# The value product of an attention stage from one float32 pass to three float16 passes

## The chip, the core and the metric

The kernel runs on one core of a Trainium2 chip. Its time is device microseconds of that core, the median of several runs; the profile is of one execution. The core's engines each work through their own instructions in order: TensorE (PE, with its weight loads as PEld), VectorE (DVE), ScalarE (ACT), GpSimd (POOL) and SyncE (SP, which issues most transfers).

## What is computed

Attention with rotary embedding over 4 batches, 8 heads, 576 positions and head size 64, then two feed-forward stages over the 2304 x 512 result: one that takes the maximum of three products, and one with x * sigmoid(x).

```python
scores = scale * np.matmul(q_rot, k_rot.transpose(0, 1, 3, 2))
scores = scores - np.max(scores, axis=-1, keepdims=True)
attn = np.exp(scores)
attn = attn / (np.sum(attn, axis=-1, keepdims=True) + 1e-09)
attn_out = np.matmul(attn, v)
...
h = np.maximum(np.maximum(x @ w1, x @ w2), x @ w3)
x = h @ w_out
...
h = x @ w_in
g = h * (1.0 / (1.0 + np.exp(-h)))
out = g @ w_out
```

## The kernel before

The attention takes the heads in pairs: 4 batches x 4 pairs. A pair's 576 queries are cut in two parts, 256 queries (two tiles of 128) and 320 (two tiles of 128 and a last one, t == 4, with the 64 left queries of both heads). That makes 20 tiles in a batch and 80 in all, and `attention` (line 480) runs them as a software pipeline with one step for each tile: the scores of tile j go to PSUM (`tile_scores`), VectorE takes their maximum (L374) and ScalarE the exponential with its sum (L381), both in `tile_max`; `tile_norm` scales tile j-1 by its sum (L390 to L393); `tile_turn` transposes the probabilities of tile j-2 on TensorE, three 128 x 128 blocks to a PSUM bank (L422; L408, L413 and L414 for the last tile), and copies each bank into the SBUF tile `pt`. Of these copies two in three are ScalarE's (L426) and one VectorE's (L428). The bank ring `ps_t` has two banks, which the turns of q and k (`qk_turn`) use as well. When a part's tiles are all turned, one step later, `av` multiplies: `xp`, one bank, gets the product of a part by one matmul of all 128 columns of the array (L437, the 64 last keys of both heads) and eight of 64 columns (L441, four blocks of keys for each of two heads, the heads in the two halves of the columns). All are float32, and each float32 matmul stands in the trace as two MATMUL records. ScalarE then writes the high float16 part of `xp` (L444) and VectorE the rest (L445); these feed the first feed-forward stage.

`load_v` brings a pair's values into a ring of six float32 tiles `vd`; `v_max` and `v_scale` measure a batch's largest value and make a power of two of it, which scales `xp` at L444 and L445. Work that is not part of the tile pipeline is put at a step by `at(step, function)`: the loads and rotations of q and k, the loads and maxima of v, and `av`.

Between the attention's steps the program places matmul groups of the first feed-forward stage (`moe1`, matmuls at L510, float16 in three passes), as soon as the batch's part is ready (`x_ready`) and at a rate of 8000 columns a step; and work that brings the weights to float16 parts (`narrowing`, `narrow_w2`, `Weights.split`, on POOL, DVE and ACT). The order of each engine's instructions is then made by a scheduler that simulates the program. After the attention come what is left of the first stage and all of the second (L778, L809). Of the second stage nothing is changed.

Of the kernel before, what the change touches and what calls it, by code (L numbers as in the profile page):

```python
# [7 lines left out]
F32 = mybir.dt.float32  # L8
F16 = mybir.dt.float16
I32 = mybir.dt.int32  # L10
U16 = mybir.dt.uint16
AF = mybir.ActivationFunctionType
ALU = mybir.AluOpType
# [4 lines left out]
P = 128  # L18
# [4 lines left out]
def fused_kernel(  # L23
# [22 lines left out]
    nc = tc.nc  # L46
    B, H, S, D = q.shape
    NP = H // 2
# [34 lines left out]
    once = right("once", 1)  # L83
# [8 lines left out]
    pt_p = right("pt", 2)  # L92
# [5 lines left out]
    cos_sb = once.tile([P, 9, D], F32, name="cos_sb")  # L98
    sin_sb = once.tile([P, 9, D], F32, name="sin_sb")

    NK, NV = 4, 6
    qd = [once.tile([P, P], F32, name=f"qd{i}") for i in range(NK)]
    kd = [once.tile([P, P], F32, name=f"kd{i}") for i in range(NK)]
    vd = [once.tile([P, 5, P], F32, name=f"vd{i}") for i in range(NV)]
    yscr = dram.tile([P, KC, NT], F32, name="yscr")

    zscr = {nm: dram.tile([P, KC * (F2 // 512) * 512], F32, name="z" + nm) for nm in ("wi", "wo")}
# [2 lines left out]
    def all_max(m):  # L110

        ps = ps_m.tile([P, 512], F32, tag="m", name="m")
        nc.tensor.transpose(ps[0:1, 0:P], m, ident)
        t = small.tile([1, 1], F32, tag="amax", name="amax")
        nc.vector.tensor_reduce(out=t, in_=ps[0:1, 0:P], op=ALU.max, axis=AX.X)
        nc.tensor.matmul(ps[:, 256:257], ones, t, start=True, stop=True)
        return ps[:, 256:257]

    def scale_of(m, n, nm, pool=None):

        pool = pool or small
        e = pool.tile([P, n], F32, tag=nm + "e", name=nm + "e")
        s = pool.tile([P, n], F32, tag=nm + "s", name=nm + "s")
        i = pool.tile([P, n], F32, tag=nm + "i", name=nm + "i")
        ei, si, ii = e.bitcast(I32), s.bitcast(I32), i.bitcast(I32)
        nc.vector.tensor_scalar(out=e, in0=m, scalar1=2.0 ** -45, scalar2=None, op0=ALU.max)
        nc.vector.tensor_scalar(out=ei, in0=ei, scalar1=EXPMASK, scalar2=None, op0=ALU.bitwise_and)
        nc.vector.tensor_scalar(out=si, in0=ei, scalar1=-1, scalar2=267 << 23, op0=ALU.mult, op1=ALU.add)
        nc.vector.tensor_scalar(out=ii, in0=ei, scalar1=13 << 23, scalar2=None, op0=ALU.subtract)
        return s, i  # L130
# [17 lines left out]
    def flat(t):  # L148
        return t.rearrange("p a b -> p (a b)")

    def split(h, l, x, s, engine="act"):

        if engine == "act":
            nc.scalar.activation(out=h, in_=x, func=AF.Copy, scale=s)
        elif engine == "pool":
            nc.gpsimd.tensor_scalar(out=h, in0=x, scalar1=s, scalar2=1.0, op0=ALU.mult, op1=ALU.mult)  # L156
        else:
            nc.vector.tensor_scalar(out=h, in0=x, scalar1=s, scalar2=None, op0=ALU.mult)
        nc.vector.scalar_tensor_tensor(out=l, in0=x, scalar=s, in1=h, op0=ALU.mult, op1=ALU.subtract)
# [85 lines left out]
    raw_t, T_t, v_t, x_t = {}, {}, {}, {}  # L245
    sv_t, cy_t = {}, {}
# [30 lines left out]

    def load_v(b, hp):

        t = vd[(NP * b + hp) % NV]  # L280
        src = v[b, 2 * hp:2 * hp + 2]
        nc.sync.dma_start(
            out=t[:, 0:4, :].rearrange("p a x -> p (a x)").rearrange("p (h c d) -> p h c d", h=2, c=4),
            in_=src[:, 0:512, :].rearrange("h (p c) d -> p h c d", c=4),
        )
        for g in range(2):
            nc.sync.dma_start(out=t[64 * g:64 * g + 64, 4, 64 * g:64 * g + 64], in_=src[g, 512:576, :])
        v_t[b, hp] = t
# [9 lines left out]
    def v_scale(b):  # L298
        ma = vmax_t.pop(b)
        m = small.tile([P, 1], F32, tag="vm1", name="vm1")  # L300
        nc.vector.tensor_reduce(out=m, in_=ma, op=ALU.max, axis=AX.X)
        sv_t[b] = scale_of(all_max(m), 1, "v")

    def qk_rope(b, hp, eng=None):
        t = raw_t[b, hp]
# [38 lines left out]

    s_t, e_t, sum_t, pt_t, exps = {}, {}, {}, {}, []
    HK = (slice(0, 576), slice(576, 1152))
    evacs = [0]

    def tile_scores(key):
        b, hp, t = key  # L350
# [16 lines left out]
    def heads(key):  # L367
        return 1 if key[2] == 4 else 2
# [18 lines left out]
    def tile_norm(key):  # L387
        e, m = e_t[key], heads(key)
        r = small.tile([P, 2], F32, tag="rec", name="rec")
        nc.scalar.activation(out=r[:, 0:m], in_=sum_t.pop(key)[:, 0:m], func=AF.Copy, bias=1e-9)  # L390
        nc.vector.reciprocal(out=r[:, 0:m], in_=r[:, 0:m])  # L391
        for g in range(m):
            nc.scalar.activation(out=e[:, HK[g]], in_=e[:, HK[g]], func=AF.Copy, scale=r[:, g:g + 1])  # L393

    def tile_turn(key):
        b, hp, t = key
        n = P
        e = e_t.pop(key)
        r = int(t > 1)
        q0, w = PARTS[r][:2]  # L400
        if (b, hp, r) not in pt_t:
            pt_t[b, hp, r] = pt_p.tile([P, 9, w], F32, tag="pt", name="pt")
        pt = pt_t[b, hp, r]
        o = P * t - q0
        if t == 4:
            tr = ps_t.tile([P, 512], F32, tag="tr", name="tr")
            for c in range(4):
                nc.tensor.transpose(tr[:, c * P:(c + 1) * P], e[:, c * P:(c + 1) * P], ident)  # L408
            t4 = tr.rearrange("p (c g q) -> p c g q", c=4, g=2)
            nc.scalar.activation(out=pt[:, 0:4, o:o + 64], in_=t4[:, :, 0], func=AF.Copy)  # L410
            nc.vector.tensor_copy(out=pt[:, 5:9, o:o + 64], in_=t4[:, :, 1])
            tr = ps_t.tile([P, 512], F32, tag="tr", name="tr")
            nc.tensor.transpose(tr[:, 0:P], e[:, 448:576], ident)  # L413
            nc.tensor.transpose(tr[0:64, P:2 * P], e[:, 512:576], ident)  # L414
            nc.scalar.activation(out=pt[0:64, 4, o:o + 64], in_=tr[0:64, P:P + 64], func=AF.Copy)
            nc.vector.tensor_copy(out=pt[64:128, 4, o:o + 64], in_=tr[64:128, 64:128])
            return
        for j in range(3):
            tr = ps_t.tile([P, 512], F32, tag="tr", name="tr")
            for i in range(3):  # L420
                c = 3 * j + i
                nc.tensor.transpose(tr[:, i * n:(i + 1) * n], e[0:n, c * P:(c + 1) * P], ident[0:n, 0:n])  # L422
            to, of = pt[:, 3 * j:3 * j + 3, o:o + n], tr[:, 0:3 * n].rearrange("p (a n) -> p a n", a=3)
            evacs[0] += 1
            if evacs[0] % 3:
                nc.scalar.activation(out=to, in_=of, func=AF.Copy)  # L426
            else:
                nc.vector.tensor_copy(out=to, in_=of)  # L428

    def av(b, hp, r):  # L430
        if hp == 0 and r == 0:
            x_t[b] = x_p[b % 2].tile([P, NP, 2, S], F16, tag="x", name="x")
        pt, vv = pt_t.pop((b, hp, r)), v_t[b, hp]
        o, n = PARTS[r][:2]
        v4 = vv[:, 0:4, :].rearrange("p a x -> p (a x)").rearrange("p (h c d) -> p h c d", h=2, c=4)
        xp = ps_x.tile([P, 512], F32, tag="xp", name="xp")
        nc.tensor.matmul(xp[:, 0:n], vv[:, 4, :], pt[:, 4, :], start=True, stop=False)  # L437
        for c in range(4):
            for g in range(2):
                r = slice(64 * g, 64 * g + 64)  # L440
                nc.tensor.matmul(xp[r, 0:n], v4[:, g, c, :], pt[:, c + 5 * g, :], start=False, stop=(c == 3))  # L441
        xh, xl = x_t[b][:, hp, 0, o:o + n], x_t[b][:, hp, 1, o:o + n]
        sv = sv_t[b][0]
        nc.scalar.activation(out=xh, in_=xp[:, 0:n], func=AF.Copy, scale=sv)  # L444
        nc.vector.scalar_tensor_tensor(  # L445
            out=xl, in0=xp[:, 0:n], scalar=sv, in1=xh, op0=ALU.mult, op1=ALU.subtract
        )

    pairs = [(b, hp) for b in range(B) for hp in range(NP)]
# [7 lines left out]
    def at(j, f, *a):  # L457
        events.setdefault(j, []).append((f, a))
# [6 lines left out]
    for i, (b, hp) in enumerate(pairs):  # L465
        u = first[b, hp]
# [6 lines left out]
    for b in range(1, B):  # L473
        u = first[b, 0]
        for hp in range(NP):
            at(u - 10 + hp if hp < 2 else u - 4, load_v, b, hp)
            at(u - 2, v_max, b, hp)
        at(u, v_scale, b)

    def attention():  # L480

# [217 lines left out]
    o = 0  # L699
    while o < NT:  # L700
        n = min(512, NT - o)
# [195 lines left out]
    for hp in range(NP):  # L897
        load_v(0, hp)
# [6 lines left out]
    for hp in range(NP):  # L905
        at(1, v_max, 0, hp)
    at(2, v_scale, 0)

    def moe_groups():
        for b in range(B):  # L910
            for half, cols, down in moe1(b, mpools):
                if down and b not in cy_t:
                    pre_down()
                    y_scale(b)
                yield b, half, cols
# [48 lines left out]
    n = 0  # L964
# [63 lines left out]
```

## Time and profile before

| | us |
|---|---|
| median of 3 runs | 1076.05 |
| lowest and highest run | 1074.24, 1076.91 |
| the profiled execution's own time | 1072.23 |
| its span, first to last instruction | 1070.5 |
| attention, first to last maximum (L374) | about 26 to 626 us of the span |

The profile gives each engine's busy time, the span in slices, the chain of work that ended last, groups of instructions by line, and waits. A duration of a matmul record runs to its modelled end; matmuls overlap, so the pace of a stream is read from the starts.

### The profile page before, as it was taken

How to read it: one execution, taken by the hardware profiler on the slowest of the kernel's cores; microseconds unless marked ns; L12 is line 12 of the kernel's file. 1: busy time of each engine (PE TensorE's matmuls, PEld its weight loads, DVE VectorE, ACT ScalarE, POOL GpSimd, SP SyncE). 2: the span in 40 equal slices, each digit the busy share in tenths (PEclk: the TensorE clock that was granted, in tenths of full speed). 3: DMA queues.
4: the chain of work that ended last, by engine and by line, in shares of the span. 5: the costliest groups of instructions: out<-in, count | busy, mean ns of one | idle time of the engine just before them, and what ended most of it. 6: DMA issues, size and time to landing. Idle time of an engine off the chain costs nothing.

```text
span 1070.5 us, 19191 instructions
## 1 busy us (share of the span) xinstructions
PE 984.0 (92%) x7554; PEld 761.6 (71%) x7554; DVE 595.0 (56%) x1078; ACT 592.0 (55%) x1298; POOL 370.2 (35%) x396
## 2 busy tenths in 40 slices
PE   2378897999998999989999999999999999999997
PEld 1245574676776677667767567778888888888887
DVE  5858667544476666476456559654532533533432
ACT  3668775646665767756666756464433433433432
POOL 1596125730115741032111211144343433433432
PEclk9678998999999999999999999998999999999999
DMA  7633022310225433223323326110100200100000
GB/s 193 204 111 111 30 90 57 82 24 1 73 85 146 122 95 90 72 73 86 122 60 89 115 68 248 49 64 1 60 10 12 60 16 6 40 21 1 21 21 20
DMA packets 81129, 76.28 MB, mean 71 GB/s; under 512 B 44944, under 2 KB 61840, under 8 KB 80528
## 3 DMA queue, kind: packets, MB, share of 16 engines
q1 hardware_dynamic: 77328, 64.77, 20.7%
q10 hardware_dynamic: 3712, 10.29, 2.9%
q8 instruction: 59, 0.97, 0.4%
q14 instruction: 30, 0.25, 0.1%
HBM read 57.21 MB, written 17.83 MB: 70 GB/s over the span
## 4 chain that ended last, share of the span: by engine, by line
PE 71%; DVE 5%; DMA 3%; POOL 1%; issue 1%; SPq 1%; ACT 1%; DVEq 0%; POOLq 0%; ACTq 0%
PE m L510 18%; PE mb L778 8%; PE m L778 8%; PE xp L441 5%; PE a L809 4%; PE c L809 4%; PE s L364 4%; PE b L809 4%; PE tr L422 4%; PE mg L510 3%; PE d L809 2%; PE xp L437 1%; PE s L361 1%; PE tr L328 1%; PE s L354 1%
## 5 line engine op out<-in xcount | busy, mean ns | idle before, releaser
L785 POOL TENSOR_TENSOR gs<-gs 128x256 f32<-128x256 f32 x144 | 131.4, 913 | 222.0 <-ACT gs L779 216.5
L510 PE MATMUL m<-x,w 128*128 128x256 f16 (+1 forms) x1380 | 197.8, 289 | 6.0 <-DVE t L528 3.2
L510 PEld LDWEIGHTS <-w 128*128 128x128 f16 x1632 | 158.6, 99 | 53.1 <-issue 13.0
L791 DVE SCALAR_TENSOR_TENSOR g<-gs,sg,g 128x768 f16<-128x768 f32 x72 | 97.9, 1362 | 173.4 <-ACT g L790 173.0
L778 PEld LDWEIGHTS <-wi 128*128 128x128 f16 x1656 | 162.0, 98 | 18.7
L809 PEld LDWEIGHTS <-g 128*128 128x128 f16 x1485 | 146.1, 99 | 21.5 <-DVE g L791 3.3
L207 POOL TENSOR_SCALAR z<-z 128x256 uint16<-128x256 uint16 x64 | 54.2, 847 | 256.6 <-DVE z L206 242.1
L374 DVE TENSOR_REDUCE nb<-s 128x2 f32<-128x1152 f32 (+1 forms) x80 | 98.7, 1234 | 63.1 <-PE s L364 48.4
L381 ACT ACTIVATE e<-s,nb 128x576 f32<-128x576 f32 x144 | 105.3, 737 | 46.3 <-DVE nb L374 42.0
L790 ACT ACTIVATE g<-gs,sg 128x768 f16<-128x768 f32 x72 | 74.9, 1041 | 72.2 <-POOL gs L785 71.1
L393 ACT ACTIVATE e<-e,rec 128x576 f32<-128x576 f32 x144 | 104.3, 768 | 17.9 <-DVE rec L391 17.7
L422 PE MATMUL tr<-ident,e 128*128 128x128 f32 x576 | 98.0, 287 | 12.1 <-ACT pt L426 3.1
L778 PE MATMUL mb<-yt,wi 128*128 128x256 f16 x828 | 95.0, 273 | 0.0
L778 PE MATMUL m<-yt,wi 128*128 128x256 f16 x828 | 94.8, 273 | 0.0
L422 PEld LDWEIGHTS tr<-ident,e 128*128 128x128 f32 x576 | 68.6, 145 | 32.8 <-ACT pt L426 5.8
L426 ACT ACTIVATE pt<-tr 128x384 f32<-128x384 f32 x128 | 61.1, 488 | 50.2 <-PE tr L422 49.8
L441 PE MATMUL xp<-pt,vd 128*64 128x256 f32 (+1 forms) x512 | 85.3, 427 | 0.0
L364 PE MATMUL s<-T 64*128 64x512 f32 (+2 forms) x384 | 82.1, 510 | 0.0
L510 PE MATMUL m<-h,wo 128*128 128x256 f16 (+1 forms) x448 | 64.9, 286 | 2.3 <-POOL wo L156 1.2
L364 PEld LDWEIGHTS s<-T 64*128 64x128 f32 x384 | 45.9, 196 | 27.3 <-issue 5.6
L779 ACT ACTIVATE gs<-mb,ch 128x512 f32<-128x512 f32 x36 | 24.7, 686 | 71.9 <-PE mb L778 71.9
L441 PEld LDWEIGHTS xp<-pt,vd 128*64 128x64 f32 x512 | 37.1, 140 | 35.0 <-issue 17.7
(199 smaller groups left out, 1500.0 us busy)
## 6 DMA issues: line engine op xcount, KB each, us to landing
z<-in_moe_w_in_dram SPq DMA_DIRECT2D x32, 256.0 KB, 3.2
z<-in_moe_w_out_dram SPq DMA_DIRECT2D x32, 256.0 KB, 3.2
w<-in_moe_w_dram ACTq DMA_DIRECT2D x6, 768.0 KB, 7.5
wo<-in_moe_w_dram ACTq DMA_DIRECT2D x6, 768.0 KB, 5.5
qk<-in_q_dram SPq DMA_DIRECT2D x32, 128.0 KB, 3.1
qk<-in_k_dram SPq DMA_DIRECT2D x32, 128.0 KB, 3.0
vd<-in_v_dram SPq DMA_DIRECT2D x16, 256.0 KB, 3.0
zwi<-z SPq DMA_DIRECT2D x32, 128.0 KB, 3.1
```

What stands on the lines that cost most here:

```text
L364: nc.tensor.matmul(s[0:n, o:o + m], qs[r], kt[r, a:a + m], start=True, stop=True)
L374: x = nc.vector.tensor_reduce(out=nb[:, 0:m], in_=s[:, 0:576 * m].rearrange("p (h k) -> p h k", h=m), op=ALU.max, axis=AX.X, negate=True)
L381: x = nc.scalar.activation(out=e[:, HK[g]], in_=s[:, HK[g]], func=AF.Exp, bias=nb[:, g:g + 1], accum_out=sm[:, g:g + 1])
L393: nc.scalar.activation(out=e[:, HK[g]], in_=e[:, HK[g]], func=AF.Copy, scale=r[:, g:g + 1])
L422: nc.tensor.transpose(tr[:, i * n:(i + 1) * n], e[0:n, c * P:(c + 1) * P], ident[0:n, 0:n])
L441: nc.tensor.matmul(xp[r, 0:n], v4[:, g, c, :], pt[:, c + 5 * g, :], start=False, stop=(c == 3))
L510: nc.tensor.matmul(ps[:, 0:n], l, r, start=(i == 0), stop=(i == len(passes) - 1))
L778: nc.tensor.matmul(ps[:, e * 256:e * 256 + 256], l, r, start=(i == 0), stop=(i == len(passes) - 1))
L785: nc.gpsimd.tensor_tensor(out=g[o], in0=g[x], in1=g[y], op=op)
L790: nc.scalar.activation(out=h, in_=x, func=AF.Copy, scale=sg)
L791: nc.vector.scalar_tensor_tensor(out=l, in0=x, scalar=sg, in1=h, op0=ALU.mult, op1=ALU.subtract)
L809: x = nc.tensor.matmul(ps, l, r, start=first, stop=last_, skip_group_check=True)
```

## The change

The value product becomes three float16 passes: high values by high probabilities, high by low, low by high. A new step `v_split` scales a pair's values and splits them into two float16 tiles (`vs`, a ring of six), on ScalarE and VectorE, at the batch's first two steps (for the first batch at steps 2 and 3); the ring of float32 tiles `vd` shrinks to four, and `v_scale` comes one step earlier. The probabilities are scaled up by 2 to the 14th through the reciprocal of their sum. Behind each turn, a new `turned` takes the bank out twice: ScalarE copies it as float16 (the high part), and VectorE then reads the same bank and subtracts that copy (the low part). So each bank has a ScalarE instruction and, behind it, a VectorE instruction, where it had one or the other. `av` has three matmuls in place of one float32 matmul, 27 instead of 9, and its results are scaled by a constant instead of a tile.

```diff
--- before.py
+++ after.py
@@ -98,10 +98,12 @@
     cos_sb = once.tile([P, 9, D], F32, name="cos_sb")
     sin_sb = once.tile([P, 9, D], F32, name="sin_sb")
 
-    NK, NV = 4, 6
+    NK, NV, NVR = 4, 6, 4
+    PSC = 2.0 ** 14
     qd = [once.tile([P, P], F32, name=f"qd{i}") for i in range(NK)]
     kd = [once.tile([P, P], F32, name=f"kd{i}") for i in range(NK)]
-    vd = [once.tile([P, 5, P], F32, name=f"vd{i}") for i in range(NV)]
+    vd = [once.tile([P, 5, P], F32, name=f"vd{i}") for i in range(NVR)]
+    vs = [once.tile([P, 2, 5, P], F16, name=f"vs{i}") for i in range(NV)]
     yscr = dram.tile([P, KC, NT], F32, name="yscr")
 
     zscr = {nm: dram.tile([P, KC * (F2 // 512) * 512], F32, name="z" + nm) for nm in ("wi", "wo")}
@@ -277,7 +279,7 @@
 
     def load_v(b, hp):
 
-        t = vd[(NP * b + hp) % NV]
+        t = vd[(NP * b + hp) % NVR]
         src = v[b, 2 * hp:2 * hp + 2]
         nc.sync.dma_start(
             out=t[:, 0:4, :].rearrange("p a x -> p (a x)").rearrange("p (h c d) -> p h c d", h=2, c=4),
@@ -300,6 +302,13 @@
         m = small.tile([P, 1], F32, tag="vm1", name="vm1")
         nc.vector.tensor_reduce(out=m, in_=ma, op=ALU.max, axis=AX.X)
         sv_t[b] = scale_of(all_max(m), 1, "v")
+
+    def v_split(b, hp):
+
+        x, t = flat(v_t[b, hp]), vs[(NP * b + hp) % NV]
+        h, l = (t[:, i].rearrange("p a x -> p (a x)") for i in range(2))
+        split(h, l, x, sv_t[b][0])
+        v_t[b, hp] = t
 
     def qk_rope(b, hp, eng=None):
         t = raw_t[b, hp]
@@ -344,7 +353,6 @@
 
     s_t, e_t, sum_t, pt_t, exps = {}, {}, {}, {}, []
     HK = (slice(0, 576), slice(576, 1152))
-    evacs = [0]
 
     def tile_scores(key):
         b, hp, t = key
@@ -387,10 +395,16 @@
     def tile_norm(key):
         e, m = e_t[key], heads(key)
         r = small.tile([P, 2], F32, tag="rec", name="rec")
-        nc.scalar.activation(out=r[:, 0:m], in_=sum_t.pop(key)[:, 0:m], func=AF.Copy, bias=1e-9)
+        nc.scalar.activation(out=r[:, 0:m], in_=sum_t.pop(key)[:, 0:m], func=AF.Copy, scale=1.0 / PSC, bias=1e-9 / PSC)
         nc.vector.reciprocal(out=r[:, 0:m], in_=r[:, 0:m])
         for g in range(m):
             nc.scalar.activation(out=e[:, HK[g]], in_=e[:, HK[g]], func=AF.Copy, scale=r[:, g:g + 1])
+
+    def turned(to, of):
+
+        h, l = to
+        nc.scalar.activation(out=h, in_=of, func=AF.Copy)
+        nc.vector.tensor_tensor(out=l, in0=of, in1=h, op=ALU.subtract)
 
     def tile_turn(key):
         b, hp, t = key
@@ -399,7 +413,7 @@
         r = int(t > 1)
         q0, w = PARTS[r][:2]
         if (b, hp, r) not in pt_t:
-            pt_t[b, hp, r] = pt_p.tile([P, 9, w], F32, tag="pt", name="pt")
+            pt_t[b, hp, r] = pt_p.tile([P, 2, 9, w], F16, tag="pt", name="pt")
         pt = pt_t[b, hp, r]
         o = P * t - q0
         if t == 4:
@@ -407,43 +421,40 @@
             for c in range(4):
                 nc.tensor.transpose(tr[:, c * P:(c + 1) * P], e[:, c * P:(c + 1) * P], ident)
             t4 = tr.rearrange("p (c g q) -> p c g q", c=4, g=2)
-            nc.scalar.activation(out=pt[:, 0:4, o:o + 64], in_=t4[:, :, 0], func=AF.Copy)
-            nc.vector.tensor_copy(out=pt[:, 5:9, o:o + 64], in_=t4[:, :, 1])
+            for g in range(2):
+                turned([pt[:, i, 5 * g:5 * g + 4, o:o + 64] for i in range(2)], t4[:, :, g])
             tr = ps_t.tile([P, 512], F32, tag="tr", name="tr")
             nc.tensor.transpose(tr[:, 0:P], e[:, 448:576], ident)
             nc.tensor.transpose(tr[0:64, P:2 * P], e[:, 512:576], ident)
-            nc.scalar.activation(out=pt[0:64, 4, o:o + 64], in_=tr[0:64, P:P + 64], func=AF.Copy)
-            nc.vector.tensor_copy(out=pt[64:128, 4, o:o + 64], in_=tr[64:128, 64:128])
+            turned([pt[0:64, i, 4, o:o + 64] for i in range(2)], tr[0:64, P:P + 64])
+            turned([pt[64:128, i, 4, o:o + 64] for i in range(2)], tr[64:128, 64:128])
             return
         for j in range(3):
             tr = ps_t.tile([P, 512], F32, tag="tr", name="tr")
             for i in range(3):
                 c = 3 * j + i
                 nc.tensor.transpose(tr[:, i * n:(i + 1) * n], e[0:n, c * P:(c + 1) * P], ident[0:n, 0:n])
-            to, of = pt[:, 3 * j:3 * j + 3, o:o + n], tr[:, 0:3 * n].rearrange("p (a n) -> p a n", a=3)
-            evacs[0] += 1
-            if evacs[0] % 3:
-                nc.scalar.activation(out=to, in_=of, func=AF.Copy)
-            else:
-                nc.vector.tensor_copy(out=to, in_=of)
+            turned([pt[:, i, 3 * j:3 * j + 3, o:o + n] for i in range(2)], tr[:, 0:3 * n].rearrange("p (a n) -> p a n", a=3))
 
     def av(b, hp, r):
         if hp == 0 and r == 0:
             x_t[b] = x_p[b % 2].tile([P, NP, 2, S], F16, tag="x", name="x")
         pt, vv = pt_t.pop((b, hp, r)), v_t[b, hp]
         o, n = PARTS[r][:2]
-        v4 = vv[:, 0:4, :].rearrange("p a x -> p (a x)").rearrange("p (h c d) -> p h c d", h=2, c=4)
+        v4 = [vv[:, i, 0:4, :].rearrange("p a x -> p (a x)").rearrange("p (h c d) -> p h c d", h=2, c=4) for i in range(2)]
         xp = ps_x.tile([P, 512], F32, tag="xp", name="xp")
-        nc.tensor.matmul(xp[:, 0:n], vv[:, 4, :], pt[:, 4, :], start=True, stop=False)
+        three = ((0, 0), (0, 1), (1, 0))
+        for i, (x, y) in enumerate(three):
+            nc.tensor.matmul(xp[:, 0:n], vv[:, x, 4, :], pt[:, y, 4, :], start=(i == 0), stop=False)
         for c in range(4):
-            for g in range(2):
-                r = slice(64 * g, 64 * g + 64)
-                nc.tensor.matmul(xp[r, 0:n], v4[:, g, c, :], pt[:, c + 5 * g, :], start=False, stop=(c == 3))
+            for i, (x, y) in enumerate(three):
+                for g in range(2):
+                    r = slice(64 * g, 64 * g + 64)
+                    nc.tensor.matmul(xp[r, 0:n], v4[x][:, g, c, :], pt[:, y, c + 5 * g, :], start=False, stop=(c == 3 and i == 2))
         xh, xl = x_t[b][:, hp, 0, o:o + n], x_t[b][:, hp, 1, o:o + n]
-        sv = sv_t[b][0]
-        nc.scalar.activation(out=xh, in_=xp[:, 0:n], func=AF.Copy, scale=sv)
+        nc.scalar.activation(out=xh, in_=xp[:, 0:n], func=AF.Copy, scale=1.0 / PSC)
         nc.vector.scalar_tensor_tensor(
-            out=xl, in0=xp[:, 0:n], scalar=sv, in1=xh, op0=ALU.mult, op1=ALU.subtract
+            out=xl, in0=xp[:, 0:n], scalar=1.0 / PSC, in1=xh, op0=ALU.mult, op1=ALU.subtract
         )
 
     pairs = [(b, hp) for b in range(B) for hp in range(NP)]
@@ -475,7 +486,9 @@
         for hp in range(NP):
             at(u - 10 + hp if hp < 2 else u - 4, load_v, b, hp)
             at(u - 2, v_max, b, hp)
-        at(u, v_scale, b)
+        at(u - 1, v_scale, b)
+        for hp in range(NP):
+            at(u + (hp > 1), v_split, b, hp)
 
     def attention():
 
@@ -905,6 +918,8 @@
     for hp in range(NP):
         at(1, v_max, 0, hp)
     at(2, v_scale, 0)
+    for hp in range(NP):
+        at(2 + hp // 2, v_split, 0, hp)
 
     def moe_groups():
         for b in range(B):
```

## Rows read from the trace of the kernel before

**Rows 1.** Page: the chain that ended last, share of the span by engine.
```profile
PE 71%; DVE 5%; DMA 3%; POOL 1%; issue 1%; SPq 1%; ACT 1%; DVEq 0%; POOLq 0%; ACTq 0%
```
**Rows 2.** Busy time in stretches: from:to and length, engines' busy us, granted clock, DMA.
```profile
20.00:60.00 40.00, 20.57 (x74) 13.86 (x74) 33.96 (x48) 21.79 (x51) 20.07 (x13) 0.66 0.58 166
60.00:120.00 60.00, 46.48 (x249) 28.05 (x249) 40.52 (x66) 47.60 (x107) 37.27 (x31) 0.89 0.33 103
120.00:200.00 80.00, 71.16 (x489) 49.36 (x489) 58.67 (x121) 52.71 (x134) 34.04 (x34) 0.96 0.23 62
200.00:640.00 440.00, 423.46 (x3004) 302.44 (x3004) 254.63 (x574) 281.70 (x759) 120.09 (x130) 0.99 0.29 83
```
**Rows 3.** Timeline of PE: start us, us, what. Each value product and the matmul behind it.
```profile
233.52 0.60 PE L437 MATMUL xp<-pt,vd 128*128 128x256 f32 x2
...
235.93 1.26 PE L510 MATMUL m<-x,w 128*128 128x320 f16 x8
...
280.31 0.70 PE L437 MATMUL xp<-pt,vd 128*128 128x320 f32 x2
...
283.25 0.45 PE L510 MATMUL m<-h,wo1f 128*128 128x320 f16 x2
```
**Rows 4.** The chain in order of time: start us, us, what. Float16 matmuls.
```profile
358.30 1.63 PE m L510 x12
...
363.32 1.31 PE m L510 x12
```
**Rows 5.** Busy time in stretches, instructions on `xp` alone: PE, PEld, DVE, ACT.
```profile
60.00:120.00 60.00, 15.49 (x71) 7.07 (x70) 1.91 (x4) 1.89 (x4) 0.89 0.33 103
120.00:200.00 80.00, 14.20 (x72) 5.97 (x72) 2.19 (x4) 2.09 (x4) 0.96 0.23 62
```
**Rows 6.** Groups by line and shape, ACT and DVE: busy us, mean ns; idle before.
```profile
L426 ACT ACTIVATE pt<-tr 128x384 f32<-128x384 f32 x128 | 61.1, 488 | 50.2 <-PE tr L422 49.8
L428 DVE COPY pt<-tr 128x384 f32<-128x384 f32 x64 | 35.2, 551 | 16.9 <-PE tr L422 16.6
L528 DVE SCALAR_TENSOR_TENSOR t<-m,t 128x320 f32<-128x320 f32 x40 | 19.5, 486 | 21.5 <-PE m L510 20.1 <-ACT t L526 1.0 <-PE tr L422 0.3
L528 DVE SCALAR_TENSOR_TENSOR t<-m,t 128x256 f32<-128x256 f32 x41 | 17.1, 416 | 6.7 <-PE m L510 4.5 <-PE m L113 1.3 <-ACT t L526 0.6
L411 DVE COPY pt<-tr 128x256 f32<-128x256 f32 x16 | 6.7, 421 | 8.4 <-ACT pt L410 8.2
L159 DVE SCALAR_TENSOR_TENSOR yt<-yr,ys,yt 128x512 f16<-128x512 f32 x16 | 12.7, 802 | 0.0
L159 DVE SCALAR_TENSOR_TENSOR w<-w,sw11s 128x768 f16<-128x768 f32 x6 | 6.1, 1010 | 1.6 <-POOL w L156 1.6
L790 ACT ACTIVATE g<-gs,sg 128x768 f16<-128x768 f32 x36 | 33.6, 935 | 1.1
```
**Rows 7.** Busy time in 20 us stretches, 120 to 640, columns as in Rows 2.
```profile
120.00:140.00 20.00, 18.61 (x141) 14.11 (x142) 16.27 (x32) 12.47 (x33) 5.45 (x6) 1.00 0.07 17
140.00:160.00 20.00, 20.00 (x152) 14.87 (x151) 12.81 (x25) 16.08 (x40) 4.18 (x3) 1.00 0.35 113
...
200.00:220.00 20.00, 19.01 (x143) 13.95 (x142) 8.62 (x14) 11.45 (x29) 12.26 (x13) 1.00 0.38 104
...
460.00:480.00 20.00, 16.12 (x128) 12.79 (x126) 15.07 (x33) 11.28 (x32) 8.13 (x9) 0.99 0.30 84
...
600.00:620.00 20.00, 17.42 (x103) 10.49 (x100) 13.15 (x34) 15.60 (x46) 4.73 (x6) 1.00 0.34 101
620.00:640.00 20.00, 18.89 (x154) 14.66 (x153) 9.72 (x32) 10.70 (x27) 1.13 (x2) 1.00 0.17 54
```
**Rows 8.** Waits of the whole span: who for whom, us, times, longest.
```profile
DVE x L445 <- ACT x L444: 17.1, 14, 2.6
```
**Rows 9.** The weight loads of the value product: duration ns min/median/max, first and last start us.
```profile
L441 PEld LDWEIGHTS xp<-pt,vd x512: 132/137/231, 61.4 to 640.7; 128*64 128x64 f32 x171
L437 PEld LDWEIGHTS xp<-pt,vd x64: 186/192/338, 58.9 to 638.4; 128*128 128x128 f32 x64
```

## The prediction

> **What bounds the kernel now.** First the chain of work that ended last: 71% of the span is PE, VectorE has 5%, ScalarE 1% [rows 1]. Then the busy time by stretch, which says where that holds [rows 2]. From 200 to 640 us, most of the attention, PE is busy 423.5 of 440 us at a granted clock of 0.99, while VectorE is at 58% and ScalarE at 64%: the matmul groups of the first feed-forward stage fill PE between the attention's steps, and PE sets the pace. Before 200 us it doesn't. From 20 to 60 PE works half the time and VectorE 85%; from 60 to 120 PE has 77%, ScalarE 79% and VectorE 68%; from 120 to 200 PE has 89% and VectorE 73%. There the weights are brought to float16, the feed-forward groups aren't ready or only just are, and the steps go as fast as VectorE, ScalarE and the transfers let them. So the question is what the change takes from PE behind 200 us and what it puts on VectorE ahead of it and beside it.
>
> **What PE saves.** A product of 256 queries takes from 233.52 to the next matmul at 235.93, 2.41 us; one of 320 takes 280.31 to 283.25, 2.94 us [rows 3]. Twelve float16 matmuls take 1.31 us at 256 columns and 1.63 at 320 [rows 4]: a step of 0.109 and 0.136 us. A float32 record is two such steps: two records on the whole array and sixteen in eight pairs, both halves of the columns at once, are 10 x 2 steps, 2.18 and 2.72 us; the other 0.23 and 0.22 are the changes between whole array and halves, which stay. Three float16 passes are 3 steps and 12 pairs, 15 steps. So a product saves five steps, 0.55 or 0.68 us, and 32 products 19.6 us. Four products of 256 lie before 120 us and four of 320 between 120 and 200 [rows 5]; the 24 left lie where PE sets the pace and save 12 x 0.55 + 12 x 0.68 = 14.7 us. The others save 4.9 us where PE mostly waits anyway.
>
> No float16 matmul of half the array stands in the trace. Its bounds: a pair in one step, as the float32 pairs go, or one after the other, two steps. I take the pair, since the row of the same form is the nearest; the other end is a rival.
>
> The weight loads speak on the side of the other end. Loading 64 columns takes 137 ns and 128 columns 192 [rows 9], 55 ns for 64 columns, and the two loads of a pair now hide under a step of 0.22 or more; the step shrinks to half. The Trainium skill, TensorEngine Tiling (Array Packing), section Restrictions and Gotchas, says that tiling the columns excludes the fast weight load, so float16 would load halves no faster than float32 does. If the two loads of a pair go one behind the other, that is 2 x 55 = 110 ns by the rows: the length of the shorter step, so by the rule as by the row the sum stays.
>
> **What VectorE gets.** All 192 banks of full tiles now end with a VectorE subtraction 384 wide from PSUM; 64 of them had a VectorE copy of 551 ns. The nearest row with a PSUM and an SBUF input is L528, 416 ns at 256 and 486 at 320, 1.09 ns an element: 556 ns at 384. 192 x 0.556 - 64 x 0.551 = 71.5 us. A last tile (16 of them) has two subtractions of 256 for a copy of 421 ns, +0.41 us, and two small ones for a small copy, about +0.3 by my estimate from the same slope: 11 us. The new split of v, 16 times 640 wide, lies between 802 ns at 512 and 1010 at 768: 0.91, 14.5 us [rows 6]. Sum: 97 us on VectorE, 82.5 of them in the turns, 1.03 us a tile.
>
> **What ScalarE gets.** 64 more copies of 488 ns, the last tiles' second copies (some 9 us, priced as VectorE's), and 16 splits of under 935 ns: 55 us at most [rows 6]. It gets less than VectorE, so I price VectorE. POOL clears two tiles fewer; SP's loads of v keep their steps, and their ring is free once the split has run, earlier than before: both nothing. `v_scale` moves up a step with its small PE and VectorE instructions; the split behind it has three steps until the batch's first product (in the first batch one or two), so its latency is hidden, and its 3.6 us a batch are counted above. Without that cover the first product would start late by them, once a batch.
>
> **Where it falls.** By 120 us four parts of two tiles have been multiplied and about ten tiles turned; four parts of three tiles follow by 200 [rows 5]. So VectorE gets 10 x 1.03 + 3.6 = 14 us in 20 to 120, 12 x 1.03 + 3.6 = 16 in 120 to 200, and 67 in 200 to 640.
>
> In 20 to 120 VectorE is busy 74.5 of 100 us [rows 2]. The cost lies between nothing, if all goes into its 25 idle us, and 14 us. I take half, 7: the first 40 us, at 85%, have little room, the rest has some.
>
> In 120 to 200 it would need 58.7 + 16 = 75 of 80 us. The highest share it holds over a long stretch is the 85% of 20 to 60 [rows 2]; at that, 75 us take 88: +8 at most, 0 at least. I take 5, nearer the upper end, since PE waits there already and its own saving of 2.7 us there is not counted.
>
> In 200 to 640 the price is what PE waits more. I sorted the 26 stretches of 20 us between 120 and 640 by VectorE's busy time [rows 7]. Twelve under 12 us (first 200 to 220, last 620 to 640): PE idle 0.2 us on average. Ten from 12 to 15 (first 140 to 160, last 600 to 620): 1.2. Four over 15 (first 120 to 140, last 460 to 480): 2.7. Of the 22 stretches behind 200, 12, 8 and 2 are of these kinds. 67 us more are 3 us a stretch; 4, 8 and 10 would be, and PE's idle time would go from 16.5 to 0.7 + 9.8 + 27.3 = 38 us: +21. That is the upper end, because stretches with a busy VectorE are also those where loads and weights are late. The lower end is 0. I take half, 10, because at 12 to 15 us half of the stretches still have PE busy without a break.
>
> Why VectorE's share should hurt at all: each of the 224 subtractions waits for ScalarE's copy of the same bank, and what stands behind it on VectorE waits too: the next tile's maximum (L374), on which the exponential and through the only score tile the next scores on PE depend, and the feed-forward stage's copies (L528), on which its two PSUM banks depend. The one pair of this form, L444 and L445, made VectorE wait 17.1 us in 14 of 32 cases [rows 8]. The transposes' two banks are held for two instructions instead of one, so PE's turns wait for them as well.
>
> **Sum.** +7 + 5 + 10 - 14.7 = +7.3 us. Behind 640 us nothing changes. The profiled execution took 1072.2 us, so 1079.5; the median of the runs shown is 3.8 above it: 1083 us.
>
> **Rivals.** The cover holds. VectorE at (254.6 + 67) / 426 = 76% and ScalarE at 74% are less than what the busiest long stretch shows, and the scheduler can order the feed-forward copies first. Then PE keeps its 14.7 us, waits 2 more behind 200 us, and the early stretches cost 2: -11, 1065 us. Against it stand the stretches over 15 us, all four with PE idle. This is the one on the other side; it decides if a VectorE busy three quarters of the time leaves PE's idle time where it is.
>
> VectorE sets the pace. All upper ends: +14 + 8 + 21 - 14.7 = +28, 1104 us. For it: 224 more waits behind ScalarE on an engine in order. Against it: the wait shrinks when VectorE comes later anyway.
>
> The halves don't overlap in float16, or their loads don't hide. Then a product is 3 + 24 = 27 steps against 20, +0.76 or +0.95 us; the 28 products behind 120 us add 12 x 0.76 + 16 x 0.95 = 24 us, with the early 7 and 5 +36: 1112 us. Against it is the float32 pace, which needs both halves at once.
>
> **How the numbers follow.** Forecast 0.42, cover holds 0.36, VectorE sets the pace 0.15, halves apart 0.07. What a measurement of this kernel can tell from no change is about 0.3%, 3.2 us. The forecast, by itself 1075 to 1092, has 0.09 inside that band; the cover's case, 1058 to 1075, has 0.06. So faster 0.30, same 0.15, slower 0.55. The range goes from 1060, the cover's case with nearly all of PE's 14.7 us, to 1106, just over the case of VectorE's pace; the halves apart stay out.
>
> **What would show it.** The product's steps: the start of L437 to the matmul behind its last half, 1.87 and 2.26 us; 2.9 or more means the halves run apart. The subtraction: mean 0.52 to 0.60 us. Early: the step at which the eighth product is done, now just before 200 us, some 12 us later. Late: PE's idle time in the 440 us of the attention's main part, 26 instead of 16.5, with waits for the subtraction's bank or L528 among its longest. I am wrong if VectorE comes to 76% there and PE's idle time stays, or if the steps before 200 us keep their times.

## The result and the profile after

The changed kernel takes 1092.5 us (median; 1090.0 to 1094.6) against 1076.5: 1.0145 times as long, with a 95% interval of 1.0107 to 1.0183. The forecast was 1083, slower, in a range of 1060 to 1106. The profiled execution took 1090.0 us with a span of 1088.2, 17.7 more than before.

The page of the changed kernel, busy time and the chain by engine:

```profile
PE 973.6 (89%) x7842; PEld 774.7 (71%) x7842; DVE 672.4 (62%) x1254; ACT 634.0 (58%) x1410; POOL 378.1 (35%) x394
...
PE 70%; DVE 7%; ACT 5%; DMA 3%; issue 2%; POOL 1%; SPq 1%; DVEq 0%; ACTq 0%; POOLq 0%
```

PE was busy 984.0 of 1070.5 us before and is 973.6 of 1088.2 now: 10 us less busy time, 28 us more idle time. VectorE is busy 77 us longer, ScalarE 42. In the chain VectorE and ScalarE have grown from 5% and 1% [rows 1] to 7% and 5%.

Busy time in the same stretches as in [rows 2], PE, PEld, DVE, ACT, POOL, then the granted clock (as a share of 2.4 GHz):

```profile
20.00:60.00 40.00, 18.32 (x63) 12.03 (x64) 34.18 (x47) 20.14 (x48) 17.86 (x12) 0.62 0.52 146
60.00:120.00 60.00, 38.29 (x221) 25.10 (x222) 47.24 (x73) 44.31 (x99) 41.77 (x33) 0.78 0.40 126
120.00:200.00 80.00, 68.08 (x517) 51.16 (x515) 64.23 (x143) 60.49 (x149) 26.08 (x24) 0.91 0.16 50
200.00:640.00 440.00, 411.03 (x3174) 306.02 (x3175) 308.76 (x695) 315.56 (x854) 131.96 (x140) 0.97 0.28 82
```

PE idles 29.0 us between 200 and 640, where it idled 16.5, and 55.3 us between 20 and 200, where it idled 41.8. The granted clock is lower in all four stretches, most from 60 to 120: 0.78 instead of 0.89.

The timeline of PE shows a product of each size (start us, us, what), as [rows 3] do for the float32 ones:

```profile
214.47 0.43 PE L448 MATMUL xp<-pt,vs 128*128 128x320 f16 x2
214.84 1.82 PE L453 MATMUL xp<-pt,vs 128*64 128x320 f16 x24
216.59 0.49 PE L369 MATMUL s<-kd,T 128*128 128x128 f32 x2
...
253.66 0.38 PE L448 MATMUL xp<-pt,vs 128*128 128x256 f16 x2
253.97 1.50 PE L453 MATMUL xp<-pt,vs 128*64 128x256 f16 x24
255.40 0.49 PE L369 MATMUL s<-kd,T 128*128 128x128 f32 x2
```

Two of the three whole-array matmuls and all 24 halves take 2.12 us at 320 and 1.74 at 256; with the third (0.136 and 0.109, it was issued a little earlier) 2.26 and 1.85. The halves do run in pairs.

The product at 214.47 is the eighth, the last of the first batch. In the kernel before it stands here:

```profile
192.00 0.70 PE L437 MATMUL xp<-pt,vd 128*128 128x320 f32 x2
192.63 2.37 PE L441 MATMUL xp<-pt,vd 128*64 128x320 f32 x16
```

The groups of the take-out and the split, as [rows 6] (line, shape, count; busy us, mean ns; idle before):

```profile
L407 DVE TENSOR_TENSOR pt<-tr,pt 128x384 f16<-128x384 f32 x192 | 104.5, 551 | 67.4 <-ACT pt L406 66.6
L406 ACT ACTIVATE pt<-tr 128x384 f16<-128x384 f32 x192 | 92.3, 488 | 51.2 <-PE tr L436 50.0
L161 DVE SCALAR_TENSOR_TENSOR vs<-vd,vs,vs 128x640 f16<-128x640 f32 x16 | 20.8, 1327 | 0.0
```

And three waits of the changed kernel (who for whom: us, times, longest), beside [rows 8]:

```profile
DVE pt L407 <- ACT pt L406: 80.6, 98, 3.1
PEld tr L436 <- DVE pt L407: 20.8, 15, 5.8
PE tr L436 <- DVE pt L407: 16.0, 11, 5.5
```

VectorE waits 81 us behind ScalarE for the high parts, and PE's turns wait for VectorE to let a bank go. The longest of these, 5.5 us, shows how it goes. The timeline of all engines around it:

```profile
496.33 0.22 ACT L406 ACTIVATE pt<-tr 64x64 f16<-64x64 f32 x1
...
497.25 1.19 DVE L161 SCALAR_TENSOR_TENSOR vs<-vd,vs,vs 128x640 f16<-128x640 f32 x1
...
498.37 0.84 DVE L208 TENSOR_SCALAR z<-z 128x256 f32<-128x256 f32 x1
...
499.33 4.17 DVE L161 SCALAR_TENSOR_TENSOR vs<-vd,vs,vs 128x640 f16<-128x640 f32 x3
...
503.53 0.23 DVE L407 TENSOR_TENSOR pt<-tr,pt 64x64 f16<-64x64 f32 x1
503.79 0.16 DVE L399 RECIPROCAL rec<-rec 128x1 f32<-128x1 f32 x1
503.81 0.90 PE L436 MATMUL tr<-ident,e 128*128 128x128 f32 x3 [5.49 <-DVE pt L407]
...
503.99 0.77 ACT L401 ACTIVATE e<-e,rec 128x576 f32<-128x576 f32 x1 [6.36 <-DVE rec L399]
```

ScalarE has copied a small bank by 496.6. The subtraction that frees it takes 0.23 us, but it stands on VectorE behind four splits of v and pieces of the narrowing, and runs at 503.5. PE waits 5.5 us for the bank, ScalarE 6.4 for the reciprocal behind it. Busy time in stretches of 4 us there, columns as above:

```profile
496.00:500.00 4.00, 2.32 (x20) 1.67 (x17) 4.00 (x7) 1.55 (x5) 3.76 (x5) 1.00 0.02 6
500.00:504.00 4.00, 0.19 (x1) 0.19 (x2) 3.94 (x6) 0.01 (x1) 3.83 (x4) 0.54 0.00 0
504.00:508.00 4.00, 4.00 (x30) 2.47 (x30) 3.97 (x8) 3.16 (x9) 0.36 (x1) 0.61 0.35 102
```

VectorE is full all the while, PE nearly empty from 500 to 504, and its granted clock is 0.54 there and 0.61 in the next stretch, when PE has work again: much of that work runs at the lower level, 1.2 GHz.

### The profile page after: what moved, and what is told of

Same layout as the page of the kernel before. It is cut to its first block, busy times and chain, and to the rows that moved or that the text cites. A ratio compares the mean times of both kernels' runs of the same rounds, so it can differ in the third digit from the quotient of the medians.

```text
span 1088.2 us, 20041 instructions
## 1 busy us (share of the span) xinstructions
PE 973.6 (89%) x7842; PEld 774.7 (71%) x7842; DVE 672.4 (62%) x1254; ACT 634.0 (58%) x1410; POOL 378.1 (35%) x394
## 3 DMA queue, kind: packets, MB, share of 16 engines
q8 instruction: 62, 1.02, 0.4%
## 4 chain that ended last, share of the span: by engine, by line
PE 70%; DVE 7%; ACT 5%; DMA 3%; issue 2%; POOL 1%; SPq 1%; DVEq 0%; ACTq 0%; POOLq 0%
PE m L523 18%; PE mb L791 8%; PE m L791 8%; PE tr L436 5%; PE a L822 4%; PE c L822 4%; PE s L372 4%; PE b L822 4%; PE xp L453 4%; PE mg L523 3%; PE d L822 2%; ACT e L389 1%; PE s L369 1%; PE s L362 1%; DMA w<-in_moe_w_out_dram 1%
## 5 line engine op out<-in xcount | busy, mean ns | idle before, releaser
L523 PE MATMUL m<-x,w 128*128 128x256 f16 (+1 forms) x1380 | 201.7, 290 | 6.8 <-ACT t L539 4.4
L407 DVE TENSOR_TENSOR pt<-tr,pt 128x384 f16<-128x384 f32 (+2 forms) x256 | 124.8, 494 | 82.4 <-ACT pt L406 80.6
L406 ACT ACTIVATE pt<-tr 128x384 f16<-128x384 f32 (+2 forms) x256 | 110.8, 440 | 67.2 <-PE tr L436 50.0
L436 PE MATMUL tr<-ident,e 128*128 128x128 f32 x576 | 101.0, 292 | 25.2 <-DVE pt L407 16.0
L436 PEld LDWEIGHTS tr<-ident,e 128*128 128x128 f32 x576 | 71.3, 149 | 43.2 <-DVE pt L407 20.8
L372 PE MATMUL s<-T 64*128 64x512 f32 (+2 forms) x384 | 85.0, 529 | 0.0
L372 PEld LDWEIGHTS s<-T 64*128 64x128 f32 x384 | 48.2, 202 | 29.4 <-issue 8.4
L453 PE MATMUL xp<-pt,vs 128*64 128x256 f16 (+1 forms) x768 | 65.9, 305 | 0.6 <-ACT pt L406 0.6
L321 POOL TENSOR_TENSOR w<-qk,sin_sb 128x384 f32<-128x384 f32 x36 | 41.1, 1150 | 71.6 <-DMA qk<-in_q_dram 66.6
```

The source lines that it names most:

```text
L372: nc.tensor.matmul(s[0:n, o:o + m], qs[r], kt[r, a:a + m], start=True, stop=True)
L406: nc.scalar.activation(out=h, in_=of, func=AF.Copy)
L407: nc.vector.tensor_tensor(out=l, in0=of, in1=h, op=ALU.subtract)
L453: nc.tensor.matmul(xp[r, 0:n], v4[x][:, g, c, :], pt[:, y, c + 5 * g, :], start=False, stop=(c == 3 and i == 2))
L523: nc.tensor.matmul(ps[:, 0:n], l, r, start=(i == 0), stop=(i == len(passes) - 1))
```

## Experiments

All ratios are to the kernel before on the same chip, with 95% intervals. The changed kernel itself was run on one chip only, so what is said beside it goes by the ratios. The code shows the main lines of each edit; "..." stands for the rest. The first four take the change apart.

**One take-out.** The banks are taken out once, as before the change; the rest of the change stays.

```diff
-        nc.scalar.activation(out=h, in_=of, func=AF.Copy)
-        nc.vector.tensor_tensor(out=l, in0=of, in1=h, op=ALU.subtract)
+        if act:
+            nc.scalar.activation(out=to[0], in_=of, func=AF.Copy)
+        else:
+            nc.vector.tensor_copy(out=to[0], in_=of)
...
```

> The changed kernel with each turned bank taken out once, as before the change (two in three by ScalarE, one by VectorE), and the low part of the probabilities left out of the result: the pass that multiplies it reads the high part again, so PE has the same 27 matmuls. Theory take-out (VectorE's 224 subtractions, with their waits behind ScalarE, are the price and PE's saving is real): under the kernel before, 1058 to 1070 us. Theory split of v (the four splits at a batch's start are the price): they are still there, 1084 to 1092. Theory no saving (float16 passes save PE little): 1074 to 1084.

1060.4 us, 0.9855 (0.9803 to 0.9907). Without the second take-out the change is 16 us faster than the kernel before, and PE is busy 22 us less than the 984.0 us there, so PE's saving is real:

```profile
PE 961.8 (91%) x7842; PEld 769.1 (73%) x7842; DVE 613.0 (58%) x1094; ACT 600.2 (57%) x1314; POOL 376.0 (35%) x394
```

**The take-out alone.** The float32 product stays; each bank gets ScalarE's copy and VectorE's subtraction.

```diff
+        nc.scalar.activation(out=to, in_=of, func=AF.Copy)
+        nc.vector.tensor_tensor(out=l, in0=of, in1=to, op=ALU.subtract)
...
-            evacs[0] += 1
-            if evacs[0] % 3:
-                nc.scalar.activation(out=to, in_=of, func=AF.Copy)
-            else:
-                nc.vector.tensor_copy(out=to, in_=of)
...
```

> The kernel before, float32 product and all, with the take-out of the changed one alone: every bank copied by ScalarE as float32 and behind it a VectorE subtraction of the same bank, into a scratch tile that nobody reads. Theory take-out: the price without PE's saving, 16 + 15 to 20 less some us for the split of v, 1098 to 1112. Theory split of v: it isn't there, 1076 to 1084. Theory no saving: the whole price and nothing more, 1086 to 1093.

1111.7 us, 1.0336 (1.0281 to 1.0391): 36 us slower, the top of what the take-out theory said. Its waits are those of the changed kernel:

```profile
DVE low L400 <- ACT pt L399: 85.8, 90, 3.2
...
PE tr L429 <- DVE low L400: 16.5, 16, 2.4
```

The take-out puts work on ScalarE too, and no run adds ScalarE's copies without VectorE's subtractions. That the price comes by VectorE rests on these waits: the longest waits of PE's turns name VectorE here and in the changed kernel.

**No low values.**

```diff
-        split(h, l, x, sv_t[b][0])
+        nc.scalar.activation(out=h, in_=x, func=AF.Copy, scale=sv_t[b][0])
...
```

> The changed kernel without VectorE's 16 subtractions of the values (1.33 us each, 20.8 in all): v_split writes the high part alone, the low part of the values is left out of the result, and the pass that multiplies it reads the high part again. Theory take-out: 1085 to 1091, a few us less than the changed kernel. Theory split of v: 1072 to 1080, back near the kernel before.

1076.1 us, 1.0004 (0.9981 to 1.0027). A miss for the take-out theory: 21 us of VectorE's time seem to be worth 15 us (1.0145 to 1.0004), as the theory of the split said. The next runs ask whether that holds.

**The splits alone**, in the kernel before, into a spare tile:

```diff
+        split(h, l, flat(v_t[b, hp]), sv_t[b][0])
...
-        at(u, v_scale, b)
+        at(u - 1, v_scale, b)
+        for hp in range(NP):
+            at(u + (hp > 1), v_split, b, hp)
...
```

> The kernel before with the 16 splits of v alone, both halves, into a spare tile that nobody reads, at the changed kernel's steps; float32 product and old take-out. Theory load with interaction (VectorE's time costs the more, the fuller it is): 1076 to 1083. Fixed price, the 16 us that leaving the low values out gave: 1086 to 1094.

1072.6 us, 0.9959 (0.9939 to 0.9979): below both ranges; nothing is lost, even a little won. So the splits show no price of their own beside the old take-out. The edit also has `v_scale` a step earlier, as the change has it; what that does alone is a run further down.

**The splits spread** over the steps:

```diff
-            at(u + (hp > 1), v_split, b, hp)
+            at(u + 2 * hp, v_split, b, hp)
...
```

> The changed kernel with the four splits of v spread over the steps: one every second step, each four steps ahead of its pair's first product, in place of two and two at the batch's first two steps. The work is the same. Theory load (VectorE's time as such is the price, wherever it lies): 1088 to 1095 us, as the changed kernel. Theory burst (four splits of 1.33 us beside the rotations and maxima at a batch's start stop the tile pipeline): 1076 to 1084, as without the low values.

1088.6 us, 1.0131 (1.0111 to 1.0152), as the changed kernel. Bursts like the one at 497 us are not the price as a whole.

**The bank free sooner.**

```diff
-        nc.vector.tensor_tensor(out=l, in0=of, in1=h, op=ALU.subtract)
+        nc.vector.tensor_tensor(out=l, in0=other, in1=h, op=ALU.subtract)
...
```

> The changed kernel with the turns' subtraction reading a float32 table in SBUF in place of the PSUM bank (the low part of the probabilities is junk, so the result is off): VectorE has as many instructions of the same width and waits for ScalarE's copy as before, but the bank is free when ScalarE has read it. Theory take-out by VectorE's load: 1086 to 1095, as the changed kernel. Theory bank (the two PSUM banks of the turns, held for two reads, stop PE): 1070 to 1080.

1084.3 us, 1.0082 (1.0051 to 1.0114), between the two theories. The wait for the bank is gone from the top of PE's waits, and another has come up, that of the feed-forward groups for VectorE's copy out of their bank:

```profile
PE s L369 <- ACT e L389: 14.5, 11, 3.3
PE m L523 <- DVE t L541: 13.0, 10, 4.3
```

VectorE's load is not the same here, though. The subtraction takes longer from SBUF, 669 ns instead of 551, and VectorE is busy 703.9 us, 31 more than in the changed kernel:

```profile
L407 DVE TENSOR_TENSOR pt<-cos_sb,pt 128x384 f16<-128x384 f32 x192 | 126.2, 669 | 45.5 <-ACT pt L406 44.9
```

With more work on VectorE and a free bank the kernel is 7 us faster than the changed one (1.0145 to 1.0082). That speaks for what waits behind the subtraction and against VectorE's busy time as the price; that VectorE's lateness comes to PE by another way once the bank is free is a reading of the two waits, and no run shows it.

**How much is order?** Two neutral edits move only the order that the scheduler makes. In the kernel before, `v_scale` one step earlier:

```diff
-        at(u, v_scale, b)
+        at(u - 1, v_scale, b)
```

> The kernel before with v_scale one step earlier, as the change has it, and nothing else: the same work in a slightly other order. Any theory in which work or load is the price: 1071 to 1080 us, as the kernel before. If it moves by 8 us or more, the order that the scheduler makes is worth as much as the differences looked at here, and single experiments of that size tell little.

1080.4 us, 1.0040 (1.0019 to 1.0061), 4 us more. The kernel with the splits alone has this edit too, and with the 16 splits on top it is 8 us faster (1.0040 to 0.9959): added work can even come with a better order. In the changed kernel, `v_scale` and the splits one step later:

```diff
-        at(u - 1, v_scale, b)
+        at(u, v_scale, b)
...
-            at(u + (hp > 1), v_split, b, hp)
+            at(u + 1 + (hp > 1), v_split, b, hp)
```

> The changed kernel with v_scale at the batch's first step, as before the change, and the splits of v one step later each; the same work, three steps at least ahead of the products still. Theory load: 1088 to 1096, as the changed kernel. If it moves by 8 us or more either way, order counts as much as load.

1100.6 us, 1.0217 (1.0192 to 1.0241), 8 us over the changed kernel with the same work. So a step of 4 to 8 us between two of these programs can be order alone. The 31 us (0.9855 to 1.0145) to 36 us (1 to 1.0336) of the take-out are well beyond that; the 7 of the freed bank aren't. The 15 us of the low values lie between, and neither the splits alone nor their spread bear them out: what they are is left open.

**Relief from GpSimd.** Four kernels take work from VectorE. The low values on GpSimd, two instructions for one:

```diff
...
+        nc.gpsimd.tensor_scalar(out=x, in0=x, scalar1=sv_t[b][0], scalar2=1.0, op0=ALU.mult, op1=ALU.mult)
+        nc.gpsimd.tensor_tensor(out=l, in0=x, in1=h, op=ALU.subtract)
```

> The changed kernel with the low part of the values made by GpSimd in two instructions (scale in place, subtract) in place of one of VectorE; nothing is left out. VectorE loses 20.8 us, GpSimd gets some 60 to 70. Both theories, load and burst: 1074 to 1082, as without the low values. If GpSimd's instructions come in the way of the rotations of q and k that it does in the same steps: 1084 to 1095.

1098.4 us, 1.0225 (1.0204 to 1.0247), slower than the changed kernel and above all the ranges. GpSimd, which rotates q and k for the coming tiles, is then busy 50 of 60 us early on, and PE falls from 38.3 to 35.7 us:

```profile
60.00:120.00 60.00, 35.70 (x208) 22.93 (x205) 40.89 (x65) 40.91 (x90) 50.28 (x41) 0.78 0.38 118
```

The first step of the second stage's narrowing on GpSimd, in the changed kernel, in the one with the low values there too, and in the kernel before:

```diff
-                nc.vector.tensor_scalar(out=self.t[i], in0=hi, scalar1=2.0 ** -112, scalar2=None, op0=ALU.mult)
+                nc.gpsimd.tensor_scalar(out=self.t[i], in0=hi, scalar1=2.0 ** -112, scalar2=1.0, op0=ALU.mult, op1=ALU.mult)
```

> The changed kernel with the narrowing's first step on GpSimd, the move that gave the kernel before 15 us; the values are split on VectorE as in the changed kernel. Theory load: VectorE is fuller here than before, so at least as much, 1070 to 1080. If the gain before was the order of one program, it need not come: 1084 to 1096.

1089.7 us, 1.0108 (1.0080 to 1.0135), 4 us under the changed kernel, with intervals that overlap.

> As the kernel with the low values on GpSimd, and the first step of the second stage's weight narrowing too (64 VectorE instructions of 0.36 us, 23 us in all, between the attention's steps 30 and 80) is GpSimd's. Theory load: each us taken from VectorE gives back half to all of itself, 1060 to 1072, faster than the kernel before. Theory burst: the narrowing lies elsewhere, 1074 to 1082.

1098.3 us, 1.0230 (1.0209 to 1.0250), as with the low values alone, and above both ranges.

> The kernel before with the same first step of the narrowing on GpSimd, as a control: its VectorE is at 58% beside a PE that is 96% busy. Theory load: nothing to gain there, 1072 to 1079. If it gains 8 us or more, the step is worth its move whatever VectorE's load is.

1058.6 us, 0.9858 (0.9836 to 0.9880), faster than both kernels. These three go against the theory that VectorE's time has one price: where VectorE is fuller the move gives 4 us or nothing, where it is at 58% it gives 15. In that last kernel PE is busy 431 of the 440 us at a clock of 1.00, though VectorE has lost only 7 us there against [rows 2]:

```profile
200.00:640.00 440.00, 431.32 (x3106) 310.54 (x3105) 247.60 (x540) 289.19 (x773) 144.80 (x196) 1.00 0.31 93
```

Its narrowing also goes less often to and fro between GpSimd and VectorE. Whether that, VectorE's time or the order of this one program gives the 15 us, these runs don't tell.

## Why the prediction was right, and where it was off

**PE's saving: right.** Forecast were 1.87 and 2.26 us a product; the timeline has 1.85 and 2.26. The halves pair up, so that rival is out. With one take-out and the splits of v in both kernels, the float16 product is worth 0.9959 to 0.9855, 11 us; with two take-outs 1.0336 to 1.0145, some 21 us, if the splits are free. The forecast counted 14.7. The two differ by 10 us, little more than the 8 that order alone moved. The prediction had a half's weights load no faster in float16 than in float32. They take 110 ns, where [rows 9] have 137:

```profile
L453 PEld LDWEIGHTS <-vs x768: 106/110/178, 72.0 to 656.5; 128*64 128x64 f16 x192
```

**VectorE's price: right in kind, too small.** The subtraction takes 551 ns (forecast 556), and the turns give VectorE 79 us more (L407's 124.8 in all, less the 45.5 of the old copies), forecast 82.5. The time that this costs was forecast at 7 + 5 + 10 = 22 us, half of most bounds. It is 31 us from the one take-out to the changed kernel, 36 by the take-out alone. That is the term that was mis-sized. The measured 1092.5 us is just above the span that the forecast called its own, 1075 to 1092. Part of the 31 to 36 may be ScalarE's: it has 42 us more to do too, and at 72% between 200 and 640 us it is as full as VectorE.

**Where it falls.** Between 200 and 640 us the forecast had PE's idle time at 26 us; it is 29.0, and VectorE's share there is 70%, not 76. It got 54 us there instead of 67, and ahead of 200 us 12.5 instead of 30: part of the attention's work comes later than the forecast had it, and other VectorE instructions got shorter by some 12 us (by the groups' sums). Still, ahead of 200 us PE idles 13.5 us more, and the forecast's own sign is off: the eighth product, 12 us later by the forecast, has its halves start at 214.8 instead of 192.6, 22 us later. The 21st maximum, two steps ahead of it, is 11 us late (191.4 instead of 180.7). So VectorE got less than half of the work that was forecast there and delayed the tiles by almost twice as much: a share of busy time, from which the prediction priced 120 to 200 us, doesn't give this delay.

**What the sum left out** is that PE's own work becomes slower. The kernel with one take-out and the changed one have the same 7842 matmul records. Of the 28.5 us between their profiled executions (spans of 1059.7 and 1088.2), PE's idle time has 16.7, which is less than the 22 of the forecast, and PE's busy time has 11.8 (961.8 to 973.6), a term that the prediction put at nothing. The clock can account for most of these: the mean granted clock is 0.964 and 0.949 (0.971 in the kernel before), and summed over the stretches at the lower level PE is busy 54 us with one take-out and 75 in the changed kernel. In the changed kernel six matmuls of the scores take 2.08 us at the lower level and 1.14 at the higher:

```profile
57.84 2.08 PE L372 MATMUL s<-T 64*128 64x512 f32 x6
...
73.73 1.14 PE L372 MATMUL s<-T 64*128 64x512 f32 x6
```

At that ratio 21 us more at the lower level cost 9.5 us, by my estimate from these rows. The take-out alone goes the same way with the records of the kernel before: PE is busy 1010.1 us instead of 984.0 and idle 102.9 instead of 86.5. There the lower level (67 us of busy time instead of 45) gives some 10 of the 26 us, and what the rest is stays open. The stretch from 500 to 508 us shows how it comes: a wait, and the lower level behind it. The Trainium skill, TensorE: Matmul & The Clock Gate, section Why this matters for your kernels, warns of idle gaps between bursts of matmuls for this reason; that stretch agrees.

**The split of v** was priced at 0.91 us and takes 1.33. The kernel with the splits alone shows why (duration ns min/median/max):

```profile
L159 DVE SCALAR_TENSOR_TENSOR spare_v<-vd,vs,spare_v x16: 877/886/1601, 59.2 to 498.4; 128x640 f16<-128x640 f32 x16
```

The six of them that ran while GpSimd computed nothing took 0.88 to 0.89 us. Ten ran beside GpSimd: six of these took 1.02 to 1.60 us, and beside the other four (0.88 to 0.89) it was GpSimd's instruction that was long, one of them 1.60 us where its like take 1.0. The Trainium skill, SBUF — State Buffer, section Who interferes with whom, has VectorE with two SBUF inputs and a GpSimd instruction that reads SBUF exclude each other; these rows agree. The forecast took the shortest rows of [rows 6] and not what lay beside them. As the splits alone cost nothing, this didn't decide the result.

**The cover of `v_split`** was given as its three steps ahead of the first product. That held for the product, for none waits for a split in the trace. What it missed is what stands behind the splits on VectorE, as at 497 us: a small subtraction and a reciprocal.

**The rivals.** That the cover holds is out: PE idles 28 us more. That VectorE sets the pace took all upper ends, 43 us, which overshoot the 31 to 36 about as far as the forecast's 22 fall short; but VectorE is at 70% behind 200 us and at 80% from 120 to 200, full only in short stretches as at 497 us: what PE sees are mostly waits in order.

## What to carry to other kernels

Taking 20 us from the busiest engine by giving 77 to one at 58% can lose when each new instruction stands between two others: here it waits for ScalarE's copy, holds PE's bank and delays the maximum behind it. Price such an instruction by what queues behind it, nearer to its upper bound, and leave room for the clock that PE's new waits cost. And in a program that a scheduler orders, make a neutral edit or two before believing any difference of their size.

## What the runs showed of the hardware

Float16 matmuls on the two halves of the array's columns run side by side as the float32 ones do: 24 of them at 256 columns take 1.43 us to the next matmul (253.97 to 255.40), 12 steps of 0.109 and the change behind them. The weight loads of the halves, 110 ns each, don't stretch the step. A load for the whole array in float16, twice the columns, takes 98 (medians).

A VectorE instruction from SBUF, 640 wide, takes 0.88 us by itself and up to 1.6 us beside GpSimd. A subtraction 384 wide takes 0.55 us with an input in PSUM and 0.67 with both in SBUF, in kernels where GpSimd works beside it.

The greatest surprise was the control: one step of a side task moved from VectorE to GpSimd made the kernel before 1.4% faster, and did next to nothing for the changed one.
